# A query matrix loaded by every eighth partition: one first load and one large load become nine loads

## The chip, the cores and the metric

The kernel runs on one core of one Trainium2 chip. The metric is the device time of one execution in microseconds (us): the median of the runs of a kernel. Beside it stands one execution taken by the hardware profiler; its span runs from its first to its last instruction. Engines are called as the profile calls them: PE does matrix products (PEld is its weight load), DVE, ACT and POOL do elementwise work, reductions and copies, and SP issues the loads. The loads themselves are moved by 16 DMA engines. The on-chip memory has 128 partitions; a tile is written as partitions x elements in each.

## The reference

Eight sequences, one token each, go through a gated mix of two branches. Branch A is attention over the last 2048 positions of a cache with 16 key/value heads and 32 query heads of width 128. Branch B is a layer norm and a two-layer network. All inputs are bf16. Cut to what matters here:

```python
g = sigmoid((x * gate_w).sum(-1, keepdims=True))          # x: 8 x 1 x 576
q = (x @ wq).reshape(B, 1, 32, 128)                        # wq: 576 x 4096
k = repeat(k_cache[:, :, 8192 - 2048:, :], 2, axis=1)      # caches: 8 x 16 x 8192 x 128
v = repeat(v_cache[:, :, 8192 - 2048:, :], 2, axis=1)
a = softmax(q k^T * 128 ** -0.5) v  @ wo                   # wo: 4096 x 576
y = layernorm(x)
b = gelu(y @ w1 + b1) @ w2 + b2                            # w1: 576 x 4608, w2: 4608 x 576
out = g * a + (1 - g) * b
```

The used part of the two caches is 134 MB, the four weight matrices together 20 MB. All of it is read once.

## The kernel before, in words

The kernel holds everything on chip in one large tile, `arena` (128 partitions). A part of it, `RAW`, has four slots; a slot takes one cache load of 4096 KB, 32 KB in each of 128 partitions, and behind the last slot lies some more room. The weights of the start use the same space: the query matrix's big part `wq_m` lies in slot 0, the hidden weights `w1_m` and `w1_r` in slot 3 and behind it, and the query matrix's last 64 rows `wq_r` behind these.

The work is written as a list of operations with costs and dependences. A small planner (`_Plan.schedule`, from L62 on) puts the operations of each engine in an order by estimated start, and `emit` writes them out with semaphore waits. Loads are operations of SP, and each names the load that it must follow (`after`), so the order of loads is fixed by hand:

1. the last 64 rows of the query matrix, `wq_r` (L407): 64 rows of 8 KB are laid on 128 partitions as halves of 4 KB, 512 KB in all;
2. the first 512 rows, `wq_m` (L408): partition p gets rows 4p to 4p + 3, one run of 32 KB, 4096 KB in all;
3. x (L410, 8 partitions), the gate's weights (L411), the two biases (L412, L413), each 9 KB or less;
4. the hidden weights, 512 rows (L416, 4608 KB) and 64 rows (L417, 576 KB);
5. the cache loads (L618), K 0, K 1, V 0, K 2, V 1 and so on, 16 of K and 16 of V, each of 4096 KB and each into the next of four slots as soon as that is free;
6. the output weights and the second network weights (L836, L865).

Loads of (1) and (2) count on one semaphore, `wq`. The query projection (L501 and the held matmuls of L175) waits for both and for x, which DVE and PE spread and transpose first (L422, L430, L461). Its five groups of matmuls read `wq_m` by its four rows of a partition and then `wq_r`. From the queries the score weights are made (L516 to L536, L629). The hidden layer (L543 and L501, then ACT and DVE from L555 to L562) waits for its weights and for the normalised x.

Then comes the stream over 16 tiles of keys and values. For each: two DVE transposes of the K tile (L718, 128x4096), 32 score matmuls (L732, L175), a DVE maximum (L645), the exponential on ACT (L649), a DVE transpose (L668) and four ACT copies (L674) that lay the probabilities out, and 64 value matmuls (L755 and, in a loop with registers, L188). A K slot is free after its second transpose, a V slot after its value matmuls. Groups of four tiles end with a small merge (L693 to L822). At the end the second network layer and the output projection are added up in one PSUM bank (L579), and L900, L901 and L903 write the result.

A load's form on the chip follows from its two access patterns: `wq_m` is a destination of 128 partitions with 16384 elements each.

Of the kernel before, what the change touches and what calls it, by code (L numbers as in the profile page):

```python
# [38 lines left out]
class _Plan:  # L39
# [16 lines left out]
    def dma(self, eng, fn, semkey, nbytes, deps=(), name=None, after=(), prio=0):  # L56
        op = _Op(eng, fn, deps, name, self.DMA_ISSUE, after=after, is_dma=True, dma_sem=semkey, nbytes=nbytes, prio=prio)
        op.idx = len(self.all)
        self.all.append(op)
        return op  # L60
# [106 lines left out]
def _pst(t):  # L167
    return t.ap().ap[0][0]
# [26 lines left out]
def build_kernel(nc, A_x, A_k_cache, A_v_cache, A_wq, A_wo, B_x, B_w1, B_b1, B_w2, B_b2, gate_w, out):  # L195
# [29 lines left out]
    with ExitStack() as es:  # L225
# [70 lines left out]
        arena = es.enter_context(nc.sbuf_tensor("arena", [128, (aoff[0] + 1) // 2], BF))  # L296
        AST = _pst(arena)
        arena_f = arena.bitcast(F32)

        def aoffs(name):  # L300
            return R[name][0] // 2
# [4 lines left out]
        def view(name, parts=128):  # L306
            o, n, dt = R[name]
            a = arena[0:parts, o // 2: o // 2 + (n * (2 if dt == BF else 4)) // 2]
            if dt == F32:
                a = a.bitcast(F32)  # L310
            return a
# [33 lines left out]
        RAW = view("RAW")  # L345
# [9 lines left out]
        wq_m = RAW[:, 0:4 * 4096].rearrange("p (t c) -> p t c", t=4)  # L355
        W1O = (ND - 1) * DE
        WQR = W1O + 4 * F + F // 2
        wq_r = RAW[:, WQR:WQR + 2048]
# [21 lines left out]
        add, dma = P.add, P.dma  # L380
# [23 lines left out]
        o_on8 = add("pool", lambda e: e.memset(ones8, 1.0), name="ones8", cost=0.15)  # L404


        d_wqr = dma("sp", lambda e: e.dma_start(wq_r, A_wq[512:576, :].rearrange("k (s c) -> (k s) c", s=2)), "wq", 64 * 8192, name="d_wqr")  # L407
        d_wqm = dma("sp", lambda e: e.dma_start(wq_m.rearrange("p t c -> p (t c)"), A_wq[0:512, :].rearrange("(p t) c -> p (t c)", t=4)), "wq", 512 * 8192, name="d_wqm", after=[d_wqr])  # L408
        dwq = [d_wqm, d_wqr]
        d_x = dma("sp", lambda e: e.dma_start(x_sb, x2), "x", 8 * D * 2, name="d_x", after=[d_wqm])  # L410
        d_gw = dma("sp", lambda e: e.dma_start(gw_sb, gate_w.partition_broadcast(1)), "g", D * 2, name="d_gw", after=[d_x])  # L411
        d_b1 = dma("sp", lambda e: e.dma_start(b1c, B_b1.rearrange("(c f) -> c f", c=FC)), "b", F * 2, name="d_b1", after=[d_gw])  # L412
# [500 lines left out]
def bass_gated_mix__sliding_block_cached__mixer_channel_mlp__decode_kernel(  # L913
    nc: bass.Bass,
    A_x: bass.AP,
    A_k_cache: bass.AP,
    A_v_cache: bass.AP,
    A_wq: bass.AP,
    A_wo: bass.AP,
    B_x: bass.AP,  # L920
    B_w1: bass.AP,
    B_b1: bass.AP,
    B_w2: bass.AP,
    B_b2: bass.AP,
    gate_w: bass.AP,
    out: bass.AP,
):
    build_kernel(nc, A_x, A_k_cache, A_v_cache, A_wq, A_wo, B_x, B_w1, B_b1, B_w2, B_b2, gate_w, out)
# [28 lines left out]
```

## Time and profile before

| | |
|---|---|
| median of 3 runs | 364.57 us (364.54 to 364.59) |
| the profiled execution: span | 363.0 us |
| median less that span | 1.57 us |
| bytes read | 154.29 MB |
| busy: PE, DVE, ACT, POOL | 82%, 64%, 46%, 6% of the span |
| cache loads, issue to landing | K 28.7 us, V 25.5 us (median) |

The page gives busy time by engine, the span in 40 slices of 9.07 us with a digit for the busy tenths of each engine, the load queues, and the chain of work that ended last, followed back from the end. A view of stretches gives, for each stretch, its length, then busy time and instructions of PE, PEld, DVE, ACT and POOL, then PE's granted clock, the busy share of the 16 DMA engines, and GB/s. A row of the DMA counts in the stretch in which it began, so a short stretch can show a share over 1. In a timeline a row has start, duration, engine, line, operation and tiles; in square brackets stands the engine's idle time before it and what ended that.

### The profile page before, as it was taken

The page shows a single profiled execution, that of the slowest core. Times are in us where ns is not written, and L with a number is a line of the kernel's source. Part 1 is how long each engine was busy: PE and PEld are TensorE (multiplying, and loading weights), DVE is VectorE, ACT ScalarE, POOL GpSimd, SP SyncE. Part 2 cuts the span into 40 slices and gives each one's busy share as a digit, 9 for nine tenths or more (in the row PEclk, how much of TensorE's full clock was granted, in tenths as well). Part 3 has the DMA queues.
Part 4 walks back from the last instruction along what each step waited for, and adds up shares of the span by engine and source line. Part 5 has one row for each costly group of instructions (what it writes and reads, how often), then busy time and mean ns, then how long its engine had stood idle before and what let it go on. Part 6 is the DMA issues. An engine that isn't in the chain of part 4 may idle for free.

```text
span 363.0 us, 4821 instructions
## 1 busy us (share of the span) xinstructions
PE 297.9 (82%) x1954; PEld 125.3 (35%) x1423; DVE 231.4 (64%) x166; ACT 168.6 (46%) x130; POOL 22.9 (6%) x52
## 2 busy tenths in 40 slices
PE   0456366999999979998897979997989698999875
PEld 0111000434252615242433417150615152436742
DVE  0452989576666694929385768566675949295720
ACT  1022106656647463663637373838374554656000
POOL 9032030000010000000100000000000000003000
PEclk9976598999999998999999989999999999999999
DMA  8999999999999999999999999999999999999996
GB/s 347 436 437 406 455 412 455 412 455 412 450 415 451 415 451 413 441 426 441 426 441 426 435 430 437 430 437 428 437 430 437 430 435 430 437 430 433 415 430 257
DMA packets 6102, 154.45 MB, mean 426 GB/s; under 512 B 694, under 2 KB 840, under 8 KB 1228
## 3 DMA queue, kind: packets, MB, share of 16 engines
q1 hardware_dynamic: 6092, 154.30, 98.8%
q8 instruction: 8, 0.13, 0.1%
q14 instruction: 2, 0.02, 0.0%
HBM read 154.29 MB, written 0.01 MB: 425 GB/s over the span
## 4 chain that ended last, share of the span: by engine, by line
DMA 56%; DVE 27%; PE 14%; issue 1%; ACT 1%; SPq 0%; POOL 0%
DMA arena<-in_A_k_cache_dram 47%; DVE arena L718 21%; PE ps L175 6%; DMA arena<-in_B_w_dram 6%; DMA arena<-in_A_x_dram 3%; DVE arena L668 2%; PE ps L188 2%; PE ps L755 2%; PE ps L732 2%; DVE arena L645 1%; PE ps L501 0%; PE ps L579 0%; DVE arena L557 0%; DVE arena L521 0%; ACT arena L536 0%
## 5 line engine op out<-in xcount | busy, mean ns | idle before, releaser
L718 DVE STREAM_TRANSPOSE arena<-arena 128x4096 f32<-128x4096 f32 (+1 forms) x34 | 141.7, 4175 | 21.9 <-DMA arena<-in_A_k_cache_dram 21.9
L674 ACT ACTIVATE arena<-arena 32x2048 bf16<-32x2048 bf16 x60 | 114.5, 1908 | 71.4 <-DVE arena L668 42.9
L175 PE MATMUL ps<-arena 128*128 128x512 bf16 (+3 forms) x531 | 136.1, 402 | 0.0
L188 PE MATMUL ps<-arena 128*128 x840 | 109.5, 277 | 7.3 <-issue 1.2
L188 PEld LDWEIGHTS ps<-arena 128*128 x840 | 81.4, 97 | 34.3 <-issue 19.0
L732 PE MATMUL ps<-arena 128*128 128x512 bf16 x128 | 51.4, 401 | 27.6 <-DVE arena L718 26.1
L645 DVE TENSOR_REDUCE arena<-ps 128x1 f32<-128x2048 f32 x16 | 36.7, 2291 | 53.8 <-PE ps L175 53.8
L732 PEld LDWEIGHTS ps<-arena 128*128 128x128 bf16 x128 | 12.5, 98 | 131.7 <-issue 75.3
L649 ACT ACTIVATE arena<-ps,arena 128x2048 bf16<-128x2048 f32 x16 | 40.7, 2543 | 0.5
L646 ACT ACTIVATE arena<-arena 128x1 f32<-128x1 f32 x16 | 3.2, 203 | 63.5 <-DVE arena L645 63.5
L755 PE MATMUL ps<-arena 128*128 128x256 bf16 x184 | 25.3, 272 | 1.1 <-DVE arena L663 1.1
L755 PEld LDWEIGHTS ps<-arena 128*128 128x128 bf16 x184 | 16.9, 99 | 18.8 <-issue 14.6
L668 DVE STREAM_TRANSPOSE arena<-arena 128x1024 f32<-128x1024 f32 x15 | 18.1, 1205 | 2.9 <-ACT arena L649 2.9
L579 PE MATMUL ps<-arena 128*8 128x288 bf16 (+1 forms) x140 | 9.6, 286 | 4.0 <-DMA arena<-in_A_wo_dram 3.3
L739 POOL MEMSET arena<- 128x4096 f32 x1 | 3.5, 3511 | 148.2 <-PE ps L175 148.2
L685 PE MATMUL ps<-arena 128*128 128x512 bf16 x16 | 6.5, 407 | 6.5 <-ACT arena L649 5.2
L629 POOL COPY arena<-arena 32x64 bf16<-32x64 bf16 x16 | 3.7, 229 | 123.3 <-PE ps L175 122.4
L901 ACT ACTIVATE arena<-ps 8x288 bf16<-8x288 f32 x1 | 0.4, 402 | 19.5 <-PE ps L579 19.5
L422 DVE COPY arena<-arena 8x128 bf16<-8x128 bf16 x2 | 0.5, 228 | 13.9 <-DMA arena<-in_A_x_dram 13.9
L579 PEld LDWEIGHTS ps<-arena 128*8 128x8 bf16 (+1 forms) x140 | 5.8, 86 | 9.9 <-DMA arena<-in_A_wo_dram 3.3
L900 DVE CAST arena<-ps 8x288 bf16<-8x288 f32 x1 | 0.4, 446 | 12.3 <-PE ps L579 12.3
L557 DVE TENSOR_TENSOR arena<-arena 128x1152 f32<-128x1152 f32 x1 | 1.4, 1358 | 9.7 <-ACT arena L555 9.7
(106 smaller groups left out, 94.0 us busy)
## 6 DMA issues: line engine op xcount, KB each, us to landing
arena<-in_A_k_cache_dram SPq DMA_DIRECT2D x16, 4096.0 KB, 28.7
arena<-in_A_v_cache_dram SPq DMA_DIRECT2D x16, 4096.0 KB, 25.5
arena<-in_B_w_dram SPq DMA_DIRECT2D x1, 4608.0 KB, 22.0
arena<-in_A_wo_dram SPq DMA_DIRECT2D x2, 2304.0 KB, 23.8
arena<-in_A_wq_dram SPq DMA_DIRECT2D x1, 4096.0 KB, 12.6
arena<-in_B_w_dram SPq DMA_DIRECT2D x1, 3456.0 KB, 24.1
arena<-in_B_w_dram SPq DMA_DIRECT2D x1, 1152.0 KB, 22.3
arena<-in_B_w_dram SPq DMA_DIRECT2D x1, 576.0 KB, 23.0
```

The lines of the kernel that those rows point to most:

```text
L175: return e.add_instruction(mybir.InstMatmult(name=nc.get_next_instruction_name(), engine=mybir.EngineType.PE, ins=[e.lower_ap(rhs), e.lowe ...
L188: return e.add_instruction(mybir.InstMatmult(name=nc.get_next_instruction_name(), engine=mybir.EngineType.PE, ins=[rhs, lhsT], outs=[e.low ...
L579: ins = e.matmul(ps[32 * j:32 * j + 8, BK_ACC, 0:JN], lhsT, rhs[:, JN * j:JN * j + JN], start=False, stop=True, skip_group_check=True, til ...
L629: return e.tensor_copy(dst, src)
L645: mx = add("dve", lambda e: e.tensor_reduce(out=k(g, MX + x), in_=scores, axis=AXL.X, op=ALU.max), deps=[qk_unit[t]], name="mx%d" % t, cos ...
L649: ex = add("act", lambda e: e.activation(out=bass.AP(arena, offset=aoffs("P"), ap=[[AST, 128], [64, 32], [1, 2], [2, 32]]), in_=ps[:, 0:4, ...
L668: pc = add("dve", lambda e: e.transpose(view("PC").bitcast(F32), view("P").bitcast(F32)), deps=[ex] + (sp_done[t - 1][0] if t else [o_acc0 ...
L674: return e.activation(out=bass.AP(arena, offset=32 * a * AST + aoffs(home) + 64 * a, ap=[[AST, 32], [256, 32], [1, 64]]), in_=bass.AP(aren ...
L685: mm = e.matmul(*args, start=True, stop=False, skip_group_check=True) if n == 0 else held_matmul(nc, e, *args, start=True, stop=False, ski ...
L718: return e.transpose(bass.AP(arena_f, offset=foffs(base) + 2048 * h0, ap=[[AST // 2, 128], [1, 2048 * nh]]), bass.AP(arena_f, offset=foffs ...
L732: mm = e.matmul(*args, start=False, stop=True, skip_group_check=True) if rc == 0 else held_matmul(nc, e, *args, stop=True, skip=True)
L755: return e.matmul(dst, bass.AP(arena, offset=aoffs(home) + 256 * q + ee, ap=[[AST, 128], [2, 128]]), slot(s).rearrange("p (r k d) -> p r k ...
```

## The change

The first 512 rows of the query matrix are loaded in eight sets. Set j holds partitions j, j + 8, ..., j + 120: 16 rows of 32 KB, 512 KB. Set 0 is the first load of the kernel. The last 64 rows are the second load, in the same form as before. Sets 1 to 7 follow, and then x and all else in the old order. Each byte goes to the place where it went before. All nine loads count on the semaphore `wq`, and the query projection waits for all of them. On PE, DVE, ACT and POOL the instructions, their waits and their order stay. On SP two issues become nine, and the order of all that follows stays.

```diff
-        d_wqr = dma("sp", lambda e: e.dma_start(wq_r, A_wq[512:576, :].rearrange("k (s c) -> (k s) c", s=2)), "wq", 64 * 8192, name="d_wqr")
-        d_wqm = dma("sp", lambda e: e.dma_start(wq_m.rearrange("p t c -> p (t c)"), A_wq[0:512, :].rearrange("(p t) c -> p (t c)", t=4)), "wq", 512 * 8192, name="d_wqm", after=[d_wqr])
-        dwq = [d_wqm, d_wqr]
+        def wq_set(j):
+            dst = bass.AP(arena, offset=j * AST + aoffs("RAW"), ap=[[8 * AST, 16], [1, 4 * 4096]])
+            src = A_wq[0:512, :].rearrange("(n p t) c -> p n (t c)", p=8, t=4)[j]
+            return lambda e: e.dma_start(dst, src)
+
+        dwq = []
+        for j in range(9):
+            if j == 1:
+                fn = lambda e: e.dma_start(wq_r, A_wq[512:576, :].rearrange("k (s c) -> (k s) c", s=2))
+            else:
+                fn = wq_set(max(0, j - 1))
+            dwq.append(dma("sp", fn, "wq", 512 * 1024, name="d_wq%d" % j, after=dwq[-1:]))
+        d_wqm = dwq[-1]
         d_x = dma("sp", lambda e: e.dma_start(x_sb, x2), "x", 8 * D * 2, name="d_x", after=[d_wqm])
```

`AST` is the number of elements of a partition of `arena`, so a step of `8 * AST` goes eight partitions on.

## The prediction

> **What bounds the kernel now.** I read the page from the top: the span, the DMA line of the 40 slices, the queues, and the chain that ended last.
>
> ```profile
> span 363.0 us, 4821 instructions
> DMA  8999999999999999999999999999999999999996
> GB/s 347 436 437 406 455 412 455 412 455 412 450 415 451 415 451 413 441 426 441 426 441 426 435 430 437 430 437 428 437 430 437 430 435 430 437 430 433 415 430 257
> DMA packets 6102, 154.45 MB, mean 426 GB/s; under 512 B 694, under 2 KB 840, under 8 KB 1228
> q1 hardware_dynamic: 6092, 154.30, 98.8%
> DMA 56%; DVE 27%; PE 14%; issue 1%; ACT 1%; SPq 0%; POOL 0%
> ```
>
> The reader is to see a kernel that is a stream of loads. The DMA digit is 9 from the second slice to the last but one, the slices between move 406 to 455 GB/s with no hole, and one queue keeps the 16 DMA engines busy for 98.8% of the span. PE, DVE and ACT have idle time; the transfer has none between its first and its last byte. So a microsecond of transfer time that is lost or won anywhere in the stream should stand in the end time almost whole. The chain in order of time says the same in another way:
>
> ```profile
> 1.71 12.15 DMA arena<-in_A_x_dram
> 79.66 25.41 DMA arena<-in_A_k_cache_dram
> 337.03 22.31 DMA arena<-in_B_w_dram
> 359.38 1.71 PE ps L579 x24
> ```
>
> It begins with the wait for x, which stands in the queue behind the query matrix, runs through compute until 79.66, then alternates between K loads and the DVE transposes that free their slots, and ends with the last weights and 1.71 us of matmuls. The compute piece from 13.89 to 79.66 does not contradict the bound: in that stretch, too, the queue is full (428 GB/s in 27 to 80, quoted below), so compute and stream run level there, and both hang on the same first loads.
>
> Now the first loads, from the timeline of the start, with the landings from the DMA view (columns of the first four lines: start, duration; the others: bytes, time from issue to landing):
>
> ```profile
> 0.80 0.39 SPq L407 DMA_DIRECT2D arena<-in_A_wq_dram  x1
> 1.25 0.41 SPq L408 DMA_DIRECT2D arena<-in_A_wq_dram  x1
> 1.71 0.37 SPq L410 DMA_DIRECT2D arena<-in_A_x_dram  x1
> 4.11 1.26 SPq L618 DMA_DIRECT2D arena<-in_A_k_cache_dram  x2
> ...
> arena<-in_A_wq_dram SPq DMA_DIRECT2D x1, 4096.0 KB, 12.6
> arena<-in_A_wq_dram SPq DMA_DIRECT2D x1, 512.0 KB, 3.3
> ...
> 13.89 0.23 DVE L422 COPY arena<-arena 8x128 bf16<-8x128 bf16 x1 [13.89 <-DMA arena<-in_A_x_dram]
> 27.11 0.12 PEld L543 LDWEIGHTS ps<-arena 4*128 4x128 bf16 x2 [1.72 <-DMA arena<-in_B_w_dram]
> ```
>
> The small rows (512 KB) land at 0.80 + 3.3 = 4.1, the big part (4096 KB) at 1.25 + 12.6 = 13.85, x right behind it, and DVE starts at 13.89. Then the hidden layer waits for its weights until 27.11. Both waits are waits on one first-in-first-out stream, so both move by what the query matrix's transfer gains or loses.
>
> ```profile
> 0.00:1.60 1.60, 0.00 (x0) 0.00 (x0) 0.00 (x0) 0.80 (x1) 0.92 (x7) 1.00 0.00 0
> 1.60:1.80 0.20, 0.00 (x0) 0.00 (x0) 0.00 (x0) 0.20 (x1) 0.20 (x2) 1.00 0.00 0
> 1.80:2.00 0.20, 0.00 (x0) 0.00 (x0) 0.00 (x0) 0.20 (x1) 0.20 (x2) 1.00 1.00 164
> 2.00:2.20 0.20, 0.00 (x0) 0.00 (x0) 0.00 (x0) 0.08 (x1) 0.20 (x2) 1.00 0.25 102
> 2.20:2.40 0.20, 0.00 (x0) 0.00 (x0) 0.00 (x0) 0.00 (x0) 0.20 (x2) 1.00 0.87 287
> 2.40:2.80 0.40, 0.00 (x0) 0.00 (x0) 0.00 (x0) 0.00 (x0) 0.40 (x3) 1.00 0.96 379
> 4.40:13.00 8.60, 0.45 (x1) 0.13 (x1) 0.00 (x0) 0.00 (x0) 5.57 (x6) 1.00 1.00 427
> 27.00:80.00 53.00, 37.45 (x215) 9.35 (x112) 39.83 (x15) 20.09 (x15) 5.58 (x12) 0.82 0.99 428
> 80.00:320.00 240.00, 215.61 (x1336) 92.72 (x971) 162.30 (x99) 133.56 (x96) 1.84 (x8) 0.99 1.00 433
> ```
>
> These are stretches of the span; the last two columns are the DMA engines' busy share and GB/s. Nothing moves before 1.8, the rate climbs for about a microsecond, and from there the big part goes at 427 GB/s, like the K and V loads later (433).
>
> **The change part by part.**
>
> The issues. Two issues for the query matrix become nine. By the rows of L407 and L408 one takes about 0.4 us and the next starts 0.45 us after it, so the ninth starts at 0.80 + 8 x 0.45 = 4.4 and x, L412 to L417 and the two K loads are issued 7 x 0.45 = 3.15 us later than now. That costs nothing: at 427 GB/s a set of 512 KB (0.524 MB) takes 1.23 us, so issues run ahead of the transfer from the second on, and x, issued at 1.71 + 3.15 = 4.9, is needed behind 4.7 MB that take till 13. If that cover were gone, the price would be the 3.15 us. Nothing else is queued on SP behind these issues that could go earlier: the next issue, a V load, waits for a released slot at 19.39 us. No instruction of PE, DVE, ACT or POOL is added, dropped or moved; the first matmul of the query projection waits for nine landings in place of two, and the last of them is the same bytes.
>
> The start. A first load of 16 rows of 32 KB stands in place of 128 rows of 4 KB. From 1.8 to 2.8 the stream moved 0.2 x (164 + 102 + 287) + 0.4 x 379 = 262 KB, where 427 GB/s would have moved 427 KB; 165 KB are missing, which is 0.39 us. If the longer rows let all engines start at once, 0.39 us is the most that the ramp returns; if the climb is the memory's own, nothing. I take -0.2.
>
> The seams. Seven more loads end inside the stream. The stretch from 80 to 320 has some 25 load ends (240 us at 9.7 us for 4.19 MB) and still runs at 433 GB/s with a busy share of 1.00, so a seam costs less than 1% of a load, 0.1 us. Seven cost 0 to 0.7; I take 0.1, since the row shows no loss at all.
>
> Where the bytes land. This is the term that decides. Now each load of more than a few KB spreads over all 128 partitions, and 16 engines move it at 427 GB/s, 26.7 GB/s for an engine and, equally, 26.7 GB/s for each sixteenth of the memory, eight partitions wide, that a wide load fills. A set writes only partitions j, j+8, ..., j+120. Two readings of the same 26.7 fit the trace:
> - The engine is what is limited to 26.7 GB/s. Then a set, with a row for each of 16 engines, goes at 427 as before, and this term is 0.
> - The way into the memory is what is limited, and the 16 rows of a set share ways two by two. Then a set goes at 8 x 26.7 = 213 GB/s. The big part is 4096 KB = 4.194 MB: 9.82 us at 427, 19.64 us at 213.5, so +9.82. The order of the sets does not help: all engines work on set 0, then on set 1, so the two engines of a pair meet in every set.
>
> ```profile
> arena<-in_A_x_dram SPq DMA_DIRECT2D x1, 9.0 KB
> arena<-in_B_b_dram SPq DMA_DIRECT2D x1, 9.0 KB
> arena<-in_A_k_cache_dram SPq DMA_DIRECT2D x16, 4096.0 KB, 28.7
> ```
>
> The nearest rows do not decide between 0 and +9.82: x (8 partitions) and the bias (4) are the only narrow loads, with 9 KB each, too little to see a rate, and the wide ones run with everything spread. I take +9.82, as the row that it is nearest to in size and row length is the K load, whose destination never takes more than 26.7 GB/s in any eight partitions; the free reading needs a place in memory to accept more than any row shows. On the reading side I expect no loss: the K loads pick 32 KB rows out of a cache spread over far more addresses than this matrix and run at 433.
>
> [...]
>
> The rest of the stream. A delay in the first 14 us meets no slack: x, the hidden layer's weights and both K loads stand behind the query matrix in one queue, the compute behind them starts that much later, and the slots come free that much later, while the stream behind stays full. The only idle transfer time is before 1.8 us and after the last weights land, and neither can absorb it. What is late next after x is the weight load that PE waits for at 27.11, late by the same amount.
>
> The sum: +9.82 - 0.2 + 0.1 = +9.7 on a span of 363.0, so a span of 372.7. The median of the runs is 364.57, 1.57 us over the span of the profiled execution (start and end outside it, unchanged), so **374.3 us**.
>
> **The rivals.**
>
> 1. The engine is the limit, and the sets cost nothing. For it: 26.7 GB/s per engine in every wide load, whatever the row length. Against it: those loads are equally wide, so the row can't tell engine from destination. Time: 364.57 - 0.2 + 0.1 = 364.5, with ends 364.57 - 0.39 = 364.2 and 364.57 + 0.7 = 365.3.
>
> 2. The other side: the start gets shorter. The first load has 16 rows in place of 128; if preparing the rows is what holds the first byte from 0.80 until 1.8, the first byte comes earlier, and the ramp's 0.39 us come back too. It needs the engines to keep their full rate (rival 1's reading), and it decides from a first byte 0.34 us earlier on, as 0.39 + 0.34 = 0.73 us is 0.2% of the time. At half of the 1.0 us between issue and first byte: 364.57 - 0.39 - 0.5 = 363.7. Against it: the issue of x, with 8 rows, takes 0.37 us and that of 128 rows 0.39, so the number of rows hardly shows.
>
> 3. Shared ways that take more than one engine's rate, or pairs that drift apart so that they meet only part of the time. The first bytes of the engines are spread over 1.8 to 2.4, half of a row's 1.23 us, so drift alone can save about 0.6 us. A way that takes one and a half engines gives 9.82 x (2/1.5 - 1) = +3.3: 367.8. Anything from +1.5 to +6.9 belongs here: 366 to 371.5.
>
> **How the numbers follow.** Forecast (half rate): 0.75, because it alone asks no part of the memory for more than the rows show; its own range is 371.5 to 377 (drift and ramp take off 1.2 at most, a pair that loses a tenth more while taking turns adds 2, with the seams' upper end). Rival 3: 0.07. Rival 1: 0.12. Rival 2: 0.06. The range 366 to 377 holds the forecast's case nearly whole and rival 3, about 0.8. A change of 0.2%, 0.73 us, is about what a measurement of this kernel can tell from none. Faster 0.06 (rival 2), within 0.2% 0.12 (rival 1), slower 0.82.
>
> **What would show it.** In the changed kernel's windows, 4.4 to about 22 should run near 213 GB/s with the busy share still near 1.00 (rows in flight, but each taking twice as long), and the later slices at 406 to 455 as now. x should reach DVE at about 13.89 + 9.7 = 23.6, the hidden layer's wait for its weights should end near 36.8, and every later piece of the chain should lie 9.7 us later, with the same lengths. The issues should be nine rows 0.45 apart. I am wrong if x still arrives near 13.9 (rival 1, or 2 if bytes flow before 1.5), if the slow stretch runs well above 213 (rival 3), or if the stream behind it shows holes or the later chain gives part of the delay back.

## The result and the profile after

| | before | changed |
|---|---|---|
| median | 364.58 us (364.54 to 364.62, 4 runs) | 375.7 us (375.45 to 376.1, 4 runs) |
| ratio | 1 | 1.0307, 95% interval 1.0295 to 1.032 |
| the profiled execution: its time, its span | 364.6, 363.0 | 376.1, 374.5 |

The changed kernel is 11.1 us slower by the medians; 9.7 had been forecast. One of the six executions of an experiment below, the alternate order, took 393.64 us, 5% above the other five, and is in neither its range nor its ratio; it is the one whose trace was kept. The page of its profile, the lines of DMA, queue and chain:

```profile
span 374.5 us, 4809 instructions
DMA  8999999999999999999999999999999999999996
GB/s 203 200 293 430 425 416 448 441 427 420 448 433 430 420 444 434 415 442 441 427 423 444 432 434 420 448 434 432 420 448 427 434 427 439 430 423 441 428 421 251
q1 hardware_dynamic: 6204, 154.30, 98.7%
DMA 49%; DVE 24%; PE 22%; issue 2%; SPq 1%; ACT 1%; POOL 0%
```

The DMA digit is the same in every slice: the 16 engines are as busy as before. But the first three slices (a slice is 9.36 us here) move 203, 200 and 293 GB/s where the old ones moved 347, 436 and 437. From the fourth to the last but one the rates are those of before (415 to 448). The digit alone would have hidden the whole loss; the line below it shows it. The same in stretches, the last two columns again being busy share and GB/s:

```profile
1.80:2.20 0.40, 0.00 (x0) 0.00 (x0) 0.00 (x0) 0.28 (x1) 0.40 (x3) 1.00 0.33 82
3.90:6.20 2.30, 0.00 (x0) 0.00 (x0) 0.00 (x0) 0.00 (x0) 2.30 (x4) 1.00 0.68 155
8.45:20.93 12.48, 0.00 (x0) 0.00 (x0) 0.00 (x0) 0.00 (x0) 1.52 (x2) 1.00 1.01 210
10.98:13.52 2.54, 0.00 (x0) 0.00 (x0) 0.00 (x0) 0.00 (x0) 0.00 (x0) 1.00 1.00 206
13.52:15.87 2.35, 0.00 (x0) 0.00 (x0) 0.00 (x0) 0.00 (x0) 0.00 (x0) 1.00 1.01 223
20.93:26.00 5.07, 0.00 (x0) 0.00 (x0) 0.07 (x1) 0.00 (x0) 0.00 (x0) 1.00 0.94 238
37.00:91.00 54.00, 37.29 (x211) 9.38 (x112) 39.10 (x15) 19.29 (x16) 7.19 (x19) 0.80 1.01 434
91.00:330.00 239.00, 213.46 (x1317) 91.66 (x962) 161.44 (x99) 134.63 (x96) 1.84 (x8) 0.99 1.00 433
```

The stretch from 8.45 to 20.93 holds five sets, 2.62 MB, at 210 GB/s with a busy share of 1.01: the engines hold rows all the time, and each row takes twice as long. From 37 on the rate is that of before. The start in the timeline, SP's issues and the first waits for landings:

```profile
0.80 0.62 SPq L410 DMA_DIRECT2D arena<-in_A_wq_dram  x1
1.48 0.56 SPq L415 DMA_DIRECT2D arena<-in_A_wq_dram  x1
2.08 4.31 SPq L410 DMA_DIRECT2D arena<-in_A_wq_dram  x7
6.43 0.53 SPq L420 DMA_DIRECT2D arena<-in_A_x_dram  x1
25.93 0.23 DVE L432 COPY arena<-arena 8x128 bf16<-8x128 bf16 x1 [25.93 <-DMA arena<-in_A_x_dram]
39.14 0.13 PEld L553 LDWEIGHTS ps<-arena 4*128 4x128 bf16 x2 [1.72 <-issue]
```

x, needed at 13.89 before, arrives at 25.93, 12.04 later. PE's hidden layer (L543 before, L553 now) starts 12.03 later, and no longer because of its weights. The chain in order of time:

```profile
6.43 19.47 DMA arena<-in_A_x_dram
126.71 28.64 DMA arena<-in_A_k_cache_dram
194.10 4.45 DVE arena L728
348.56 22.27 DMA arena<-in_B_w_dram
370.87 1.75 PE ps L589 x24
```

Two pieces of before that belong beside the second and third of these:

```profile
115.15 28.60 DMA arena<-in_A_k_cache_dram
182.52 4.45 DVE arena L718
```

A K load comes onto the chain at 126.71 for the first time; before it did at 79.66. Until then the chain runs through compute, which started 12.04 late, while the stream of loads is late by less. The chain's share of DMA fell from 56% to 49% by this, and that of PE rose from 14% to 22%. From 126.71 on each piece lies about 11.5 later than its counterpart: 11.56 for that K load, 11.58 for the DVE transpose at 194.10, 11.53 for the last weights (348.56 in place of 337.03). So half a microsecond of the delay was given back, and what stands at the end is the delay of the stream (in the profiled execution 376.1 - 364.6 = 11.5).

### The profile page after: what moved, and what is told of

Same layout as the page of the kernel before. It is cut to its first block, busy times and chain, and to the rows that moved or that the text cites. A ratio compares the mean times of both kernels' runs of the same rounds, so it can differ in the third digit from the quotient of the medians.

```text
span 374.5 us, 4809 instructions
## 1 busy us (share of the span) xinstructions
PE 295.2 (79%) x1935; PEld 125.2 (33%) x1423; DVE 231.3 (62%) x166; ACT 168.6 (45%) x130; POOL 22.9 (6%) x52
## 4 chain that ended last, share of the span: by engine, by line
DMA 49%; DVE 24%; PE 22%; issue 2%; SPq 1%; ACT 1%; POOL 0%
DMA arena<-in_A_k_cache_dram 38%; DVE arena L728 18%; PE ps L175 9%; PE ps L188 6%; DMA arena<-in_B_w_dram 6%; DMA arena<-in_A_x_dram 5%; PE ps L742 3%; PE ps L765 2%; DVE arena L678 2%; SPq L410 1%; DVE arena L655 1%; PE ps L589 0%; PE ps L511 0%; DVE arena L567 0%; DVE arena L531 0%
## 5 line engine op out<-in xcount | busy, mean ns | idle before, releaser
L742 PE MATMUL ps<-arena 128*128 128x512 bf16 x122 | 48.3, 396 | 19.0 <-DVE arena L728 17.3
L695 PE MATMUL ps<-arena 128*128 128x512 bf16 x11 | 4.4, 399 | 5.2 <-ACT arena L659 5.2
```

Source lines behind the costliest of these rows:

```text
L695: mm = e.matmul(*args, start=True, stop=False, skip_group_check=True) if n == 0 else held_matmul(nc, e, *args, start=True, stop=False, ski ...
L742: mm = e.matmul(*args, start=False, stop=True, skip_group_check=True) if rc == 0 else held_matmul(nc, e, *args, stop=True, skip=True)
```

## The experiments

The theory: a row of 32 KB goes through one of several ways into the memory, and a load's rate is set by how many ways its rows reach at a time. That there are 16 ways was assumed, and 26.7 GB/s for each is an estimate, the 427 GB/s of the kernel before over 16; that four neighbouring partitions use one way was assumed too. No view shows a way: the runs can show only whether the rates come out so. The rivals: a price for each load (or for each load with few rows), and the reading of rows that lie 256 KB apart. All kernels start from the changed kernel, but for the one with the big part first, which starts from the kernel before. The instructions of PE, DVE, ACT and POOL are the same in each; in the two runs that part reading from landing, and in the one behind them, the query matrix stands rearranged, so the queries are other numbers. Each was measured beside the kernel before on the same chip. That gave 364.53 us beside the columns, the 16 neighbours, the spread sets of 32 and the big part first; 364.6 beside every second partition, reading and landing apart and half the dose; and 364.59 beside the other four. Of each edit the lines that matter are shown; where only lines with + stand, they take the place of the set's `dst` and `src`, and `...` stands for further lines.

**Nine loads, but every set on all partitions.**

```diff
-            dst = bass.AP(arena, offset=j * AST + aoffs("RAW"), ap=[[8 * AST, 16], [1, 4 * 4096]])
-            src = A_wq[0:512, :].rearrange("(n p t) c -> p n (t c)", p=8, t=4)[j]
+            dst = RAW[:, 2048 * j:2048 * j + 2048]
+            src = A_wq[0:512, :].rearrange("(p t) c -> p (t c)", t=4)[:, 2048 * j:2048 * j + 2048]
```

> Eight sets again, nine loads of 512 KB in the same order on the same queue, but a set is 4 KB of each of the 128 partitions in place of 32 KB of 16. Theory (the landing costs: a set that reaches only half of the ways into the memory goes at half rate): the first 13 us run at about 427 GB/s again, x reaches DVE near 13.9, and the time is 364.6, within 0.5. Rival (nine loads in place of two cost something each, some 1.3 us): the time stays near 375.7.

Measured: 365.56 us, ratio 1.0029 (1.0017 to 1.004). The stretches of this run:

```profile
2.20:3.20 1.00, 0.00 (x0) 0.00 (x0) 0.00 (x0) 0.00 (x0) 1.00 (x5) 1.00 0.77 254
5.00:13.00 8.00, 0.45 (x1) 0.13 (x1) 0.00 (x0) 0.00 (x0) 4.98 (x6) 1.00 1.03 419
```

419 GB/s: ten of the eleven microseconds are gone with the same number of loads, bytes and issues. The 1.0 us that is left is twice the margin I gave; eight times as many rows of 4 KB, and a slower climb at the start (254 GB/s from 2.2 to 3.2, where the kernel before moved 381), may share it, and this run does not part them. It bounds the price of seven more loads from above.

**Sets of 16 neighbours.**

```diff
-            dst = bass.AP(arena, offset=j * AST + aoffs("RAW"), ap=[[8 * AST, 16], [1, 4 * 4096]])
-            src = A_wq[0:512, :].rearrange("(n p t) c -> p n (t c)", p=8, t=4)[j]
+            dst = bass.AP(arena, offset=16 * j * AST + aoffs("RAW"), ap=[[AST, 16], [1, 4 * 4096]])
+            src = A_wq[0:512, :].rearrange("(p n t) c -> p n (t c)", p=8, t=4)[j]
```

> Eight sets of 16 partitions and 32 KB rows again, but each set is 16 partitions next to each other. Theory, with four neighbours on one way into the memory: 4 of 16 ways are reached, a quarter of the rate, the big part takes 39 us in place of 9.8, so 364.6 + 29.5 = 394, and up to 398 if all of it is as much dearer as in the changed kernel (11.1 measured for 9.8 worked out). Rival 1 (a load with one row for each engine has a price of its own, wherever it lands): 375.7. Rival 2 (the reading of rows 256 KB apart is slow): these rows lie next to each other, so 364.6.

Measured: 391.16 us, ratio 1.0732 (1.0716 to 1.0749). Its stretch of the sets, and the wait for x:

```profile
13.00:37.00 24.00, 0.00 (x0) 0.00 (x0) 0.00 (x0) 0.00 (x0) 0.00 (x0) 1.00 0.96 109
```

```profile
40.99 0.23 DVE L432 COPY arena<-arena 8x128 bf16<-8x128 bf16 x1 [40.99 <-DMA arena<-in_A_x_dram]
```

A quarter of the rate: 109 GB/s, where the kernel before moved the big part at 427. Size of load, number of rows and row length are as in the changed kernel. The reading differs too, one block in place of every eighth row; but a run below, "landing as changed", reads the same blocks, lands on every eighth partition and takes 375.04 us, so between these two only the place of landing differs. Both rivals would have been far below. The total, +26.6, is less than 394 had said; if the sets follow each other on other ways, they can overlap a little at each passage, but that is argued and no view shows it (see the alternate order below).

**Four sets of 32 rows, spread or together.**

```diff
+            dst = bass.AP(arena, offset=j * AST + aoffs("RAW"), ap=[[4 * AST, 32], [1, 4 * 4096]])
+            src = A_wq[0:512, :].rearrange("(n p t) c -> p n (t c)", p=4, t=4)[j]
...
-        for j in range(9):
+        for j in range(4+1):
```

and, for the neighbours,

```diff
+            dst = bass.AP(arena, offset=32 * j * AST + aoffs("RAW"), ap=[[AST, 32], [1, 4 * 4096]])
+            src = A_wq[0:512, :].rearrange("(p n t) c -> p n (t c)", p=4, t=4)[j]
...
-        for j in range(9):
+        for j in range(5):
```

> Four sets of every fourth partition, 32 rows of 32 KB each (1024 KB). A set now reaches every group of four partitions, so all the ways. Theory, if two rows of a way are given to the same engine or to engines at different times: full rate, 364.6, within 0.7. Theory, if each engine gets two rows that lie next to each other in the set and engines that share a way keep in step: half rate, 374 to 376. Rival (one row for each engine and load has a fixed price of 1.3 us, here four times and for two rows): 364.6 + 5.5 = 370.

> Four sets of 32 rows of 32 KB as in the run with every fourth partition (365.2), but each set on 32 partitions that lie together: 8 groups of four. Theory (what counts is the number of ways that a set reaches): half rate, 364.6 + 9.8 = 374.4, within 1.5. Rival (32 rows, two for each engine, are enough for the full rate): 365.2.

Measured: spread 365.21 us, ratio 1.0019 (1.0009 to 1.0028); together 375.25 us, 1.0288 (1.0272 to 1.0304). The spread one's stretch, then that of the neighbours:

```profile
5.00:13.00 8.00, 0.45 (x1) 0.13 (x1) 0.00 (x0) 0.00 (x0) 4.99 (x6) 1.00 1.05 451
```

```profile
5.00:20.00 15.00, 0.45 (x1) 0.13 (x1) 0.00 (x0) 0.00 (x0) 4.98 (x6) 1.00 0.96 210
```

Equal loads, equal rows, and 10 us between them from the spacing. The reading is spaced along with the landing in this pair, but that weighs little: with the landing on every eighth partition, reading whole blocks or every eighth row made 0.7 us (375.04 below, against 375.7). Every fourth partition is spread enough (365.21 us), every eighth is not (375.7). (Rows count where they begin, so 451 in a short stretch is no rate above the usual.)

Side by side, 16 neighbours went at 109 GB/s, every eighth partition and 32 neighbours at 210, and every fourth at the full rate: a quarter, a half and the whole of 427. The quarter for 16 neighbours and the half for 32 are what the theory had worked out, with its assumed four neighbours to one of 16 ways.

**Every second partition of 32.**

```diff
+            dst = bass.AP(arena, offset=(32 * (j // 2) + j % 2) * AST + aoffs("RAW"), ap=[[2 * AST, 16], [1, 4 * 4096]])
+            src = A_wq[0:512, :].rearrange("(b n h t) c -> b h n (t c)", b=4, h=2, t=4)[j // 2, j % 2]
```

> Eight sets of 16 rows of 32 KB, each on every second partition of 32 that lie together. Theory, with four neighbours on one way: 8 groups of four are reached, two rows in each, so half rate as in the changed kernel, 374.5 to 376.5. Rival (what counts is how many partitions a set spans, 121 in the changed kernel, 31 here): a quarter of the rate or worse, 394 or more.

Measured: 375.87 us, ratio 1.031 (1.0293 to 1.0328), and a stretch at half the rate:

```profile
8.00:20.00 12.00, 0.00 (x0) 0.00 (x0) 0.00 (x0) 0.00 (x0) 2.00 (x2) 1.00 1.04 216
```

A span of 31 partitions costs what a span of 121 does, 375.87 us against 375.7. That fits four neighbours on one way.

**The big part first, in one load.**

```diff
-        d_wqr = dma("sp", lambda e: e.dma_start(wq_r, A_wq[512:576, :].rearrange("k (s c) -> (k s) c", s=2)), "wq", 64 * 8192, name="d_wqr")
-        d_wqm = dma("sp", lambda e: e.dma_start(wq_m.rearrange("p t c -> p (t c)"), A_wq[0:512, :].rearrange("(p t) c -> p (t c)", t=4)), "wq", 512 * 8192, name="d_wqm", after=[d_wqr])
+        d_wqm = dma("sp", lambda e: e.dma_start(wq_m.rearrange("p t c -> p (t c)"), A_wq[0:512, :].rearrange("(p t) c -> p (t c)", t=4)), "wq", 512 * 8192, name="d_wqm")
+        d_wqr = dma("sp", lambda e: e.dma_start(wq_r, A_wq[512:576, :].rearrange("k (s c) -> (k s) c", s=2)), "wq", 64 * 8192, name="d_wqr", after=[d_wqm])
...
+        d_wqm = d_wqr
```

> Two loads as in the kernel before, but the big part (rows of 32 KB) first and the small rows second. Only the ramp is tried: if long rows at the start return what the climb of the rate loses, 364.57 - 0.39 = 364.2; if the climb is there for any first load, 364.6. By the changed kernel, whose first bytes moved 0.2 to 0.4 us later than before, 364.6 is the likelier.

Measured: 364.82 us, ratio 1.0008 (0.9999 to 1.0017). The gain of the ramp that the change could have had is not there; if anything the long rows at the start cost a little (364.82 us against 364.53). x in this run:

```profile
14.31 0.23 DVE L423 COPY arena<-arena 8x128 bf16<-8x128 bf16 x1 [14.31 <-DMA arena<-in_A_x_dram]
```

That is 0.42 later than in the kernel before.

**Reading and landing apart.** The first run reads the changed kernel's rows and lands on all partitions; the second reads a block and lands as the changed kernel does.

```diff
+            dst = RAW[:, 2048 * j:2048 * j + 2048]
+            src = A_wq[0:512, :].rearrange("(n p t) (s c) -> p n (t s) c", p=8, t=4, s=2)[j]
```

```diff
+            dst = bass.AP(arena, offset=j * AST + aoffs("RAW"), ap=[[8 * AST, 16], [1, 4 * 4096]])
+            src = A_wq[0:512, :].rearrange("(p n t) c -> p n (t c)", p=8, t=4)[j]
```

> The sets read the same 16 rows of 32 KB, 256 KB apart, as in the changed kernel, but land as 4 KB in each of 128 partitions, so the query matrix stands rearranged and the queries are other numbers. Theory (landing): 364.6, within 0.5. Rival (the reading of every eighth row is what is slow): 375.7.

> The other half of the pair: the sets read one block of 512 KB each and land on every eighth partition as in the changed kernel, so the query matrix's rows are permuted and the queries are other numbers. Theory (landing): 375.7, within 0.7. Rival (reading): 364.6.

Measured: landing as changed 375.04 us, ratio 1.0284 (1.0267 to 1.0301); reading as changed 373.01 us, 1.0229 (1.0212 to 1.0246). The landing alone is enough for nearly all of the loss, 10.4 of 11.1 us, and the rate in its sets is that of the changed kernel:

```profile
8.00:20.00 12.00, 0.00 (x0) 0.00 (x0) 0.00 (x0) 0.00 (x0) 1.97 (x2) 1.00 1.01 210
```

But the other run should have been near 365 and was 8.4 slower, against my theory as I had put it: all partitions, and still

```profile
5.00:20.00 15.00, 0.45 (x1) 0.13 (x1) 0.00 (x0) 0.00 (x0) 5.00 (x6) 1.00 1.04 251
```

251 GB/s. Either reading every eighth row has a cost of its own, or all partitions of a load are not reached at a time. The next run told these apart.

**A block read, in pieces of the same order.**

```diff
+            dst = RAW[:, 2048 * j:2048 * j + 2048]
+            src = A_wq[64 * j:64 * j + 64, :].rearrange("(q m) (s c) -> m s q c", q=8, s=2).rearrange("m s q c -> (m s) q c")
```

> The run that read every eighth row and landed on all partitions took 373.0, against the theory. Here a set reads one block of 512 KB and lands as 4 KB in each of 128 partitions; only the order of the pieces is such that the source keeps two dimensions of 16 and 8, as in that run (the query matrix stands rearranged, the queries are other numbers). Theory (the 16 engines get eight neighbouring partitions each, and engines that share a way keep in step): near 373 again, 371 to 375. Rival (there it was the reading of rows 256 KB apart): 365.6, as with the sets of columns.

Measured: 372.41 us, ratio 1.0216 (1.02 to 1.0231), and 256 GB/s in the same stretch:

```profile
5.00:20.00 15.00, 0.45 (x1) 0.13 (x1) 0.00 (x0) 0.00 (x0) 4.98 (x6) 1.00 1.03 256
```

So it was not the distance of the rows read: a block of 512 KB read whole is as slow (256 GB/s, against 251), as soon as the source is written as 16 x 8 pieces. What is shown is that the form of the source changes the rate of a load that covers all partitions (419 GB/s with the columns, 256 here). That the engines then get eight neighbouring partitions each, and meet in pairs, is the explanation that predicted it; no view shows which engine wrote where. The sets of every fourth partition limit it: for engines that get neighbouring rows and keep in step their expectation gave 374 to 376, and they took 365.21. If the explanation holds, it holds for this form of source only; the cause stays open.

**Half the dose.**

```diff
+            dst = bass.AP(arena, offset=j * AST + aoffs("RAW"), ap=[[8 * AST, 16], [1, 2 * 4096]])
+            src = A_wq[0:512, :].rearrange("(n p t) c -> p n (t c)", p=8, t=4)[j][:, 0:8192]
...
+        dwq.append(dma("sp", lambda e: e.dma_start(RAW[:, 8192:16384], A_wq[0:512, :].rearrange("(p t) c -> p (t c)", t=4)[:, 8192:16384]), "wq", 512 * 4096, name="d_wq9", after=dwq[-1:]))
```

> Half the dose: the first 16 KB of each row go in eight sets of every eighth partition (256 KB a set), the other 16 KB of all 128 partitions in one load behind them. Theory (a rate that is halved): half of the cost, 364.6 + 5.5 = 370.1, within 0.8. Rival (a fixed price for each set): 375 to 376.

Measured: 369.68 us, ratio 1.0139 (1.0122 to 1.0156). 5.1 us for half the bytes against 11.1 for all, with the same eight sets: the cost goes by bytes, and a price for each set that would make up the loss is out. The two parts of the run, sets and then the one load:

```profile
5.00:12.00 7.00, 0.45 (x1) 0.13 (x1) 0.00 (x0) 0.00 (x0) 4.97 (x6) 1.00 1.02 215
13.00:18.00 5.00, 0.00 (x0) 0.00 (x0) 0.00 (x0) 0.00 (x0) 0.00 (x0) 1.00 0.99 400
```

**The sets in another order, and the small rows first.** Two runs on the rest, the difference of 11.1 and the 9.8 that had been worked out.

```diff
-                fn = wq_set(max(0, j - 1))
+                fn = wq_set((0, 0, 4, 1, 5, 2, 6, 3, 7)[j])
```

> The changed kernel with its sets in the order 0, 4, 1, 5, 2, 6, 3, 7. If sets 0 to 3 reach one half of the ways and 4 to 7 the other, as the one quicker set in the trace (2.35 us in place of 2.53, the first of the other half) suggests, there are seven passages from half to half in place of one, and each lets the leading engines run on free ways for 0.18 us: 375.7 - 6 x 0.18 = 374.6, within 0.4. Rival (each set has its own mixture of ways, or the quicker set was chance): 375.7.

```diff
-            if j == 1:
+            if j == 0:
...
-                fn = wq_set(max(0, j - 1))
+                fn = wq_set(j - 1)
```

> The changed kernel with the small rows as the first load again and the eight sets behind them. It tells what of 11.1 us belongs to the place of the first set: the first byte came 0.38 us later than before, and the small rows took 0.3 us in place of 0.16 a row (8 rows for an engine, about 1 us) behind it. If both come from the set ahead of them: 375.7 - 0.4 - 0.7 = 374.6, within 0.4. If the halved rate alone makes the 11.1: 375.7.

Measured: the alternate order has a ratio of 1.0281 (1.0267 to 1.0295), 374.35 to 375.29 us with a median of 374.74; its slowest is below the changed kernel's fastest, 375.45, though that was measured at another time. Its trace bears it out: five sets one after the other take 11.73 us, and one of them 2.35.

```profile
8.36:20.09 11.73, 0.00 (x0) 0.00 (x0) 0.00 (x0) 0.00 (x0) 1.61 (x2) 1.00 1.01 224
8.36:10.71 2.35, 0.00 (x0) 0.00 (x0) 0.00 (x0) 0.00 (x0) 1.61 (x2) 1.00 1.01 223
```

In the changed kernel five sets took 12.48 us, and only the one at the passage from sets 0 to 3 to sets 4 to 7 took 2.35, the two ahead of it 2.53 and 2.54. This fits two halves that use different ways, with a little overlap at each passage; the trace has the times of the sets, not the ways. The small rows first gave 375.1 us (374.17 to 375.83), ratio 1.0289 (1.0272 to 1.0306): 0.6 less than the changed kernel by the medians, but the two spreads overlap, so this one stays open.

## Why the prediction was right

- **The bound.** Right in the main. 11.5 of the 12.0 us by which x came later in the profiled execution are in its end. The other half microsecond was given back, which the prediction had named as a sign of being wrong, and the pieces of the chain did not keep their lengths. Compute was held up more than the stream, and so it, not the loads, carried the chain until 126.71 in place of 79.66. The marks on the way were missed by more than the total: x came at 25.93, where 23.6 was forecast, and the hidden layer started at 39.14, where 36.8 was.
- **Where the bytes land.** Right in kind: the place of landing sets the rate, and it halves, 210 GB/s against 427 (rival 1 fell with the first slices; the runs with 32 rows and with every second partition show that it is the place, and the half dose that it goes by bytes). In size it was a little dearer: 210 GB/s in place of 213, so 4.194 MB take 20.0 us and the term is +10.15 in place of +9.82. But the reason given from the rows does not lead there. A set puts one row into each run of eight partitions, so at the full rate it would ask no more than 26.7 GB/s of any eight, which is just what the K load shows; the free reading needed nothing new by that row. That rows eight partitions apart share ways two by two was assumed, and neither a row of the kernel before nor a later run shows it: what the runs show is the rate by the place of landing, 210 GB/s on every eighth partition or on 32 neighbours, 109 on 16 neighbours, the full rate on every fourth. As far as the rows go, the choice of +9.82 over 0 was luck.
- **The start.** The wrong sign. -0.2 was taken for longer rows at the start; the first bytes were fewer (82 GB/s from 1.8 to 2.2, which is a single row of 32 KB, where the rows of before, 164 and 102, make 133), and long rows first, on all partitions, gave +0.3 (-0.04 to +0.6). Rival 2 had no ground: the first issue took 0.62 us with 16 rows, 0.39 with 128.
- **The seams.** 0.1 was taken; nine loads with full landing cost at most 1.0, five spread ones 0.7. No run measures the seam alone, and the upper bound of 0.7 may have been nearer than the value taken.
- **The issues.** Nine rows, but 0.62 us apart, not 0.45 (7 in 4.31 us), so x was issued at 6.43, not 4.9. It stayed hidden, as said: the sets ahead of x moved until after 21 us.
- **What the sum left out.** Loads next to a set moved less as well: the small rows, behind set 0, 155 GB/s from 3.9 to 6.2, and set 7 and the first hidden rows behind it together 238 from 20.93 to 26. This can make up the rest of 11.1 - 9.7, but so can the start and the seams: +10.15 and the 1.0 us that nine loads with full landing cost come to 11.15. No run parts them, and the run with the small rows first did not settle their share.
- **Drift (rival 3).** Small, as bounded: one quicker set, 2.35 us at the only passage between the halves, and some 0.9 us when there are seven passages. So the order of the sets does help a little, where the prediction said that it does not. Its lower end for half rate, 371.5, does not follow from its own terms either: 374.3 less 1.2 is 373.1.

## What to carry to other kernels

Cutting a load by partitions cost 11.1 us here, although the pieces were large, their rows long and the engines all busy: look at the GB/s line, not the busy digit, since rows that take twice as long still count as busy (a share of 1.01 at 210 GB/s, of 1.00 at 427). Of the sets tried here, every fourth partition went at the full rate (365.21 us in all, against 364.53), while every eighth, every second of 32, and 32 neighbours went at half of it (210, 216 and 210 GB/s) and 16 neighbours at a quarter (109). Whether any choice of 16 partitions would go at the full rate is not shown. In this kernel, which is one stream of loads, 11.5 of the 12.0 us lost at the start stood in the end.

## What the runs showed of the hardware that was not expected

A load that covers all 128 partitions fell to 251 and 256 GB/s when its source was written as 16 x 8 pieces of 4 KB, while pieces in one even step ran at 419; the K and V loads, whose source also has two dimensions (32 x 4), run at 433 (from 91 to 330 in the changed kernel). Why is open. And the first issue, a load of 16 rows, took longer on spaced partitions than on neighbours, 0.62 us against 0.39; the run "landing as changed" has the 0.62 as well, and it reads the same blocks as the run with 16 neighbours, whose first issue is this:

```profile
0.80 0.39 SPq L410 DMA_DIRECT2D arena<-in_A_wq_dram  x1
```
